# Top-k attention and a sigmoid-gated MLP in one kernel: moving a score unit, a pair of bounds, and the PSUM home of three MLP units

## The chip, the cores and the metric

The kernel runs on one core of one Trainium2 chip. The metric is the device time of one execution in microseconds (us). Engine names follow the profile: PE is TensorE, PEld its weight load, DVE is VectorE, ACT is ScalarE, POOL is GpSimd, SP issues most of the DMAs.

## The reference

```python
# q, k, v: (8, 8, 576, 64); w_in: (512, 2048); w_out: (2048, 512); all float32
scores = matmul(q, k.transpose(0, 1, 3, 2)) / sqrt(64)
kth = partition(scores, -32, axis=-1)[..., -32:-31]   # the 32nd largest of each row
scores = where(scores >= kth, scores, -1e9)
attn = exp(scores - max(scores)); attn = attn / (sum(attn) + 1e-9)
x = matmul(attn, v)                                   # -> transposed to (4608, 512)
h = x @ w_in
out = (h * sigmoid(1.702 * h)) @ w_out
```

Each row of 576 scores keeps its 32 largest values; the rest get weight zero. The attention output of all eight heads of a token is one row of the MLP's input.

## The kernel before, in words

**Slots.** A *slot* is 128 query rows of two heads. There are 8 x 18 = 144 of them. For each slot PE computes two 128x576 score tiles (`scores`, L282) into PSUM, ACT copies them to SBUF (`copy_scores`, L294), DVE finds the 32nd largest value of each row, ACT cuts the scores at that value and takes the exponential with its row sum (`exponentials`, L397 and L400), the exponentials are transposed, and PE multiplies them with v.

**Three ways through a slot.** Slots 0 to 11 search the full rows on DVE (`topk`, L304 and L307), and transpose on PE (`turn`, L448, L451), with a diagonal matrix of 1/sum as moving operand, which POOL makes (`divide`, L413). From slot 12 on (`PAIRED`) the search works on pairs: `pair_up(n)` takes the larger of each two scores on DVE (`greater`, L323) and the smaller on POOL (`lesser`, two instructions, L326 and L327), and `topk_of_pairs` searches both (L344, L347). From slot 12 on (`SETTLED`) the exponentials also leave by DMA (`split`, L470 and L472) and come back transposed by DMA (L478); the sums are inverted on DVE (`invert`, L429, L431), spread by POOL (`wide`, L433), and multiplied in after the product with v (L527, L538, L944, L552). The bounds of the exponentials come from POOL: `cut` and `low` (L388, L389) for slots below 12, `low` (L377) later.

**The MLP.** Finished blocks of 128 tokens go through it in *units*: `hidden` (L591) makes a 128x512 piece of h in one PSUM bank, `tanh` (L613, and L616 for a copy of h) reads it on ACT, `gate` multiplies on POOL (L625, L626), and `project` (L646) adds the unit's part to the block's output in another bank, `po`. When all parts are in, ACT brings it out (`leave`, L654). Where two blocks are ready, a unit is *double*: it works on both at once, with half the columns of each, and two `po` banks are in use.

**PSUM.** The banks are split into four pools: `ps_s` (scores, two tiles of two banks), `ps_t` (two banks, tag `tp`: transposes, products with v, and some units), `ps_h` (one bank, units) and `ps_p` (one bank, `po`). The second `po` of a double unit lives in `ps_h`. Which of `ps_t` and `ps_h` a unit takes is decided in `hidden`: double units, and units that come while `pos["other"]` is set, take `ps_t`, the others take what the caller says. A tile waits for the last reader of the tile that had its bank before.

**Order.** Nothing is reordered after the program: inside `manual_schedule` each engine runs its instructions in the order in which the code emits them, and waits by semaphores. `slot(n)` emits one slot (n up to 12), `two_slots(n)` emits two (n = 13, 15, 17, ...), with the search of slots n and n+1. Of a call of `two_slots` the order on PE is: `hidden`, `project`, transposes of new q and k where they are due, `sum_rows` (L527), `scores(n+2)`, products with v (L538), `scores(n+3)`, `hidden`, `project`. On ACT `copy_scores(n+2)` follows the two instructions of `tanh` and the copies of transposed q and k (L218, L222, L224). `pair_up(n+1)` sits inside the search of slot n, at its 15th instruction, so the search of slot n goes on only when the scores of slot n+1 have been copied. The call with n = 13 (`opens`) puts `scores(15)` first.

The weights of the MLP are rounded in pieces during the first twelve slots; the last instructions of a piece are two on POOL (L144, L147), emitted while the next slot searches (`finish_one`).

Of the kernel before, what the change touches and what calls it, by code (L numbers as in the profile page):

```python
# [30 lines left out]
def kernel(  # L31
# [53 lines left out]
    SETTLED = 12  # L85
    PAIRED = 12
# [19 lines left out]
    ps_t = pool("ps_t", 2, space=PSUM)  # L106
# [274 lines left out]
    def bounds(n):  # L381

        if n >= PAIRED:
            return lows(n)
        top = st[n]["top"]
        cut = st[n]["cut"] = small.tile([P, 2], F32, name="cut")
        low = st[n]["low"] = small.tile([P, 2], F32, name="low")
        nc.gpsimd.tensor_scalar(cut[:], top[:, :, TOPK - 1], -1.0, None, op0=ALU.mult)  # L388
        nc.gpsimd.tensor_tensor(out=low[:], in0=top[:, :, TOPK - 1], in1=top[:, :, 0], op=ALU.subtract)  # L389
# [182 lines left out]
            self.left = list(range(FC))  # L572
            self.done = 0

    pos = {"other": False}
    ready = []
    to_gate, gated, to_project = [], [], []

    def hidden(into=None):
        if not ready:  # L580
            return
        blocks = ready[:2]
        many = len(blocks)
        fs = blocks[0].left[: G // many]
        first, step = min(x.place for x in blocks), abs(blocks[0].place - blocks[-1].place) or 1
        blocks = sorted(blocks, key=lambda x: x.place)
        into = ps_t if many > 1 or pos["other"] else into
        ph = (into or ps_h).tile([P, G * P], F32, name="ph", tag="tp" if into else "ph")
        for i, f in enumerate(fs):
            for c in range(CC):  # L590
                nc.tensor.matmul(  # L591
                    ph[:, i * many * P : (i + 1) * many * P],
                    lhsT=win[:, c, f * P : (f + 1) * P],
                    rhs=xs[:, first : first + step * (many - 1) + 1 : step, c, :],
                    start=(c == 0),
                    stop=(c == CC - 1),
                )
        to_gate.append((ph, fs, blocks))
        for x in blocks:
            x.left = [f for f in x.left if f not in fs]  # L600
        if many > 1:
            pos["other"] = True
        while ready and not ready[0].left:
            free.append(ready.pop(0).place)
            if len(ready) < 1 or len(ready[0].left) == FC:
                pos["other"] = False
# [58 lines left out]
    in_use = []  # L665
# [121 lines left out]
    def slot(n):  # L787

        todo = later.pop(n, [])
        for fn, args in todo:  # L790
            if fn is not prepare and fn is not prepare_by_dma:
                fn(*args)
        preparing = [(fn, args) for fn, args in todo if fn is prepare or fn is prepare_by_dma]
        some = [round_piece(x) for x in by_slot.get(n, [])] if n else early
        if n == 0:
            for piece in some:
                piece["low"]()
                piece["sign"]()
        else:
            bounds(n - 1)  # L800

            exponentials(n - 1, bring_all if n % 4 == 1 else lambda: None)
            copy_scores(n + 1)
            bring_all()
            while signs:
                signs.pop(0)()
            if 1 < n <= TURNS:
                turn_main(n - 2)
                turn_ends(n - 2)
            for piece in some:  # L810
                piece["size"]()
            tanh(False)
        for i, op in enumerate(topk_of_pairs(n) if n >= PAIRED else topk(n)):
            op()
            if i == 2:
                for _ in range(min(3 if n >= TURNS else 6, len(unfinished))):
                    finish_one()
            if i == 5:
                if n > 0:
                    divide(n - 1)  # L820
                while unfinished:
                    finish_one()
            if i == 10:
                gate(False)
        for piece in some:
            piece["shift"]()
            unfinished.extend(piece["finish"])
        if n < NP:
            for fn, args in preparing:
                fn(*args)  # L830
        if n >= TURNS:
            turn_main(n - 1)
            turn_ends(n - 1)
        if n > 0:
            for piece in some:
                piece["low"]()
        scores(n + 2)
        if n == SETTLED:
            copy_scores(n + 2)
        if n == 0:  # L840
            return
        for i, piece in enumerate(some):
            if n == TURNS and i > 0:
                signs.append(piece["sign"])
            else:
                piece["sign"]()
        idle = not ready and n < TURNS
        if 1 < n <= TURNS:
            values(n - 2, put_off if n == TURNS else None)
        if n >= TURNS:  # L850
            values(n - 1, put_off)
        if n >= NP:
            for fn, args in preparing:
                fn(*args)
        if n > PROJECTS and may_project(2):
            project()
        if idle:
            stay_warm(8)
        hidden()
# [12 lines left out]
    def two_slots(n):  # L872

        first, second = [later.pop(m, []) for m in (n, n + 1)]
        live = lambda m: 0 <= m < N
        aside = n < N

        def begin(todo):
            for fn, args in todo:
                if fn is not prepare and fn is not prepare_by_dma:  # L880
                    fn(*args)

        def prepare_some(todo):
            for fn, args in todo:
                if fn is prepare or fn is prepare_by_dma:
                    fn(*args)

        def find(m):
            for i, op in enumerate(topk_of_pairs(m) if live(m) else [lambda: None] * 23):
                op()  # L890
                if i == 8 and m % 2:
                    invert(m - 2)
                if i > 1 and unfinished:
                    finish_one()

        def project_one():
            if may_project(0):
                project(True)

        def measure(m):  # L900
            if live(m):
                bounds(m)
            gate(aside)

        opens = n == SETTLED + 1
        begin(first)
        measure(n - 1)
        if opens:
            scores(n + 2)
            bring_all()  # L910
        if live(n - 1):
            exponentials(n - 1)
            split(n - 1)
        if opens:
            copy_scores(n + 2)
            tanh(aside)
        find(n)
        hidden(ps_t if opens else None)
        project_one()
        tanh(aside)  # L920
        prepare_some(first)
        held = [m for m in (n - 3, n - 2) if live(m) and "rows" in st[m]]
        o = ps_t.tile([P, 2, 2, P], F32, name="o", tag="tp") if held else None
        for i, m in enumerate(held):
            sum_rows(m, o[:, i, 0, :])
        if live(n + 2) and not opens:
            scores(n + 2)
            copy_scores(n + 2)
        leave_all()
        for i, m in enumerate(held):  # L930
            values_at(m, o[:, i, 1, :])
        if live(n - 1):
            turn_by_dma(n - 1)
        while turns:
            turns.pop(0)()
        if live(n + 3):
            scores(n + 3)
        begin(second)
        measure(n)
        def bring():  # L940
            if not held:
                return
            x = raws.tile([P, 2, 2, P], F32, name="x", tag="raw")
            nc.scalar.copy(out=x[:], in_=o[:])  # L944
            for i, m in enumerate(held):
                x_of(m, x[:, i, 1, :], x[:, i, 0, :])

        if live(n):
            exponentials(n, bring)
        else:  # L950
            bring()
        if live(n):
            split(n)
            turn_by_dma(n)
        hidden(ps_t)
        if live(n + 3):
            copy_scores(n + 3)
        tanh(aside)
        prepare_some(second)
        project_one()  # L960
        leave_all()
        find(n + 1)

    with tc.manual_schedule():
        opening()
        for n in range(SETTLED + 1):
            if n == PAIRED:
                pair_up(n)
            slot(n)
        for n in range(SETTLED + 1, N + 4, 2):  # L970
            two_slots(n)
        while ready or to_gate or gated or to_project:
            last_slot()
# [30 lines left out]
```

## Time and profile before

| what | value |
|---|---|
| median of the three runs (1479.12, 1480.97, 1481.0) | 1480.97 us |
| the profiled execution: its time, its span | 1481.2 us, 1479.4 us |
| PE, PEld busy | 1436.7 us (97%), 1019.3 us (69%) |
| DVE, ACT, POOL busy | 1331.9 (90%), 1173.7 (79%), 860.2 us (58%) |
| mean granted TensorE clock | 0.987 |
| chain that ended last, by engine | PE 89%, DVE 6%, ACT 3% |

The span runs from the first to the last instruction; the time is 1.8 us longer. "x" counts instructions, "[0.69 <-ACT ob L654]" behind a row means that the engine had been idle for 0.69 us and that the instruction of line 654 on ACT released it. A row with x32 merges 32 records, and its duration goes from the start of the first to the end of the last; matmuls overlap at their ends, so the step from one row's start to the next row's start is the cleaner measure. Slot 12 lies at about 145 to 161 us of the span, the call of `two_slots` with n = 15 at about 188 to 207 us.

### The profile page before, as it was taken

The page shows a single profiled execution, that of the slowest core. Times are in us where ns is not written, and L with a number is a line of the kernel's source. Part 1 is how long each engine was busy: PE and PEld are TensorE (multiplying, and loading weights), DVE is VectorE, ACT ScalarE, POOL GpSimd, SP SyncE. Part 2 cuts the span into 40 slices and gives each one's busy share as a digit, 9 for nine tenths or more (in the row PEclk, how much of TensorE's full clock was granted, in tenths as well). Part 3 has the DMA queues.
Part 4 walks back from the last instruction along what each step waited for, and adds up shares of the span by engine and source line. Part 5 has one row for each costly group of instructions (what it writes and reads, how often), then busy time and mean ns, then how long its engine had stood idle before and what let it go on. Part 6 is the DMA issues. An engine that isn't in the chain of part 4 may idle for free.

```text
span 1479.4 us, 29105 instructions
## 1 busy us (share of the span) xinstructions
PE 1436.7 (97%) x9696; PEld 1019.3 (69%) x9696; DVE 1331.9 (90%) x4541; ACT 1173.7 (79%) x1865; POOL 860.2 (58%) x1119
## 2 busy tenths in 40 slices
PE   7789899999999999999999999999999999999998
PEld 5667656777666667777666667777766667777665
DVE  7999889999999999999999999999999999999910
ACT  6998588878788888888878787888878788877730
POOL 3777555655666666565666666555666666565510
PEclk8899999999999999999999999999999999999999
DMA  7451256776768677676767676676777766644430
GB/s 244 135 156 52 56 155 182 201 186 172 176 185 201 168 188 183 178 187 164 183 184 202 168 181 185 176 188 171 182 177 192 201 169 186 148 124 130 129 86 15
DMA packets 516311, 242.04 MB, mean 164 GB/s; under 512 B 452672, under 2 KB 490560, under 8 KB 516160
## 3 DMA queue, kind: packets, MB, share of 16 engines
q1 hardware_dynamic: 515728, 239.89, 61.8%
q8 instruction: 76, 1.25, 0.4%
q14 instruction: 75, 0.61, 0.1%
q10 hardware_dynamic: 432, 0.30, 0.1%
HBM read 45.09 MB, written 102.24 MB: 100 GB/s over the span
## 4 chain that ended last, share of the span: by engine, by line
PE 89%; DVE 6%; ACT 3%; issue 1%; POOL 0%; POOLq 0%; DVEq 0%; ACTq 0%
PE ph L591 33%; PE po L646 32%; PE s_ps L282 11%; PE o L538 10%; DVE top L304 3%; DVE left L307 2%; PE tp L448 1%; PE o L527 1%; ACT pr L400 1%; ACT sc L294 0%; PE o L503 0%; ACT sc L397 0%; PE none L169 0%; DVE win L152 0%; DVE top L344 0%
## 5 line engine op out<-in xcount | busy, mean ns | idle before, releaser
L591 PEld LDWEIGHTS ph<-xT,win 128*128 128x128 f32 x3520 | 483.9, 191 | 90.1 <-issue 56.2
L591 PE MATMUL ph<-xT,win 128*128 128x128 f32 (+1 forms) x3520 | 537.8, 309 | 3.4 <-ACT ob L654 2.1
L646 PE MATMUL po<-wout,th 128*128 128x512 f32 x1152 | 518.4, 593 | 1.1 <-ACT ob L654 1.1
L646 PEld LDWEIGHTS po<-wout,th 128*128 128x128 f32 x1152 | 213.2, 190 | 214.5 <-issue 207.3
L344 DVE MAX8 top<-left 128x8 f32<-128x288 f32 x792 | 325.5, 446 | 0.0
L294 ACT ACTIVATE sc<-s_ps 128x576 f32<-128x576 f32 x288 | 171.2, 647 | 141.5 <-PE s_ps L282 141.5
L470 ACT COPY sc<-pr 128x2304 uint16<-128x2304 uint16 x132 | 278.8, 2112 | 4.2
L552 POOL TENSOR_TENSOR xT<-x 128x128 f32<-128x128 f32 (+1 forms) x148 | 60.8, 433 | 298.0 <-ACT x L944 298.0
L347 DVE MATCH_REPLACE8 left<-top,left 128x288 f32<-128x288 f32 x528 | 229.7, 443 | 0.0
L326 POOL TENSOR_TENSOR lesser<-sc,greater 128x576 int32<-128x576 int32 x132 | 186.3, 1411 | 71.7 <-DVE greater L323 65.9
L400 ACT ACTIVATE pr<-sc,low 128x576 f32<-128x576 f32 x288 | 221.4, 778 | 0.0
L397 ACT ACTIVATE sc<-sc,cut 128x576 f32<-128x576 f32 x288 | 208.1, 779 | 7.8 <-POOL cut L388 7.7
L344 DVE MAX8 top<-lesser 128x8 f32<-128x288 f32 x528 | 213.9, 446 | 0.0
L327 POOL TENSOR_TENSOR lesser<-lesser,sc 128x576 int32<-128x576 int32 x132 | 186.3, 1411 | 10.4
L282 PE MATMUL s_ps<-qk_t 64*128 64x288 f32 (+1 forms) x1280 | 185.0, 436 | 0.2 <-ACT qk_t L218 0.2
L626 POOL TENSOR_TENSOR th<-th,h 128x512 f32<-128x512 f32 x128 | 163.1, 1274 | 10.8 <-POOL th L625 0.2
L323 DVE TENSOR_TENSOR greater<-sc 128x576 f32<-128x576 f32 x132 | 101.0, 765 | 53.4 <-ACT sc L294 52.6
L625 POOL TENSOR_SCALAR th<-th 128x512 f32<-128x512 f32 x128 | 79.0, 617 | 120.0 <-ACT th L613 119.8
L538 PE MATMUL o<-pt,v_l 128*64 128x128 f32 (+1 forms) x2368 | 143.8, 265 | 0.0
L538 PEld LDWEIGHTS o<-pt,v_l 128*64 128x64 f32 x2368 | 120.1, 137 | 25.7 <-issue 23.6
L282 PEld LDWEIGHTS s_ps<-qk_t 64*128 64x128 f32 (+1 forms) x1280 | 100.6, 180 | 41.5 <-issue 22.5
L613 ACT ACTIVATE th<-ph 128x512 f32<-128x512 f32 x144 | 85.9, 597 | 51.1 <-PE ph L591 44.1
(83 smaller groups left out, 1461.3 us busy)
## 6 DMA issues: line engine op xcount, KB each, us to landing
rows<-sc SPq DMA_DIRECT2D x132, 576.0 KB, 3.1
qk_rows<-halves SPq DMA_DIRECT2D x48, 256.0 KB, 2.8
qk_l<-in_q_dram SPq DMA_DIRECT2D x64, 128.0 KB, 2.9
raw<-in_moe_w_in_dram SPq DMA_DIRECT2D x16, 512.0 KB, 4.6
v_l<-in_v_dram SPq DMA_DIRECT2D x32, 256.0 KB, 3.2
raw<-in_moe_w_out_dram SPq DMA_DIRECT2D x16, 512.0 KB, 3.5
out_dram<-ob SPq DMA_DIRECT2D x32, 256.0 KB, 2.8
qk_l<-in_k_dram SPq DMA_DIRECT2D x62, 128.0 KB, 2.8
```

The costliest lines, as they stand in the source:

```text
L282: nc.tensor.matmul(ps[i][rows, c, 0:HALF], lhsT=qT[b, hps[p]][on, cols], rhs=kT[b, hps[p]][on, FIRST[i] + c * HALF : FIRST[i] + (c + 1) * ...
L294: nc.scalar.mul(out=to, in_=ps[i][:, :, 0:HALF], mul=SCALE)
L326: nc.gpsimd.tensor_tensor(out=whole, in0=a.bitcast(I32), in1=greater[n][:].bitcast(I32), op=ALU.subtract)
L327: nc.gpsimd.tensor_tensor(out=whole, in0=whole, in1=b.bitcast(I32), op=ALU.add)
L344: nc.vector.max(found(r, i, True), src[:, i, :])
L347: nc.vector.match_replace(to[:, i, :], found(r, i), src[:, i, :], LOWEST)
L397: nc.scalar.activation(sc[:, i, :], sc[:, i, :], AF.Prelu, bias=cut[:, i : i + 1], alpha=HUGE)
L400: nc.scalar.activation(pr[:, i * S : (i + 1) * S], sc[:, i, :], AF.Exp, bias=low[:, i : i + 1], accum_out=den[:, i : i + 1],)
L470: nc.scalar.copy(out=halves, in_=pr[:].bitcast(U16).rearrange("p (k h) -> p h k", h=2))
L538: nc.tensor.matmul(o[j * D : (j + 1) * D, cols], lhsT=main[:, j, c, :] if c < NF else tail[:, j, :], rhs=pt[:, MAIN[j] + c if c < NF else ...
L591: nc.tensor.matmul(ph[:, i * many * P : (i + 1) * many * P], lhsT=win[:, c, f * P : (f + 1) * P], rhs=xs[:, first : first + step * (many - ...
L646: nc.tensor.matmul(x.po[:], lhsT=gT[:, i * P : (i + 1) * P], rhs=wout[:, f, :], start=(x.done == 0), stop=(x.done == FC - 1))
```

## The change

Four edits.

1. `pair_up(12)` moves from ahead of `slot(12)` to behind `bounds(11)` in it. On POOL `cut` and `low` of slot 11 now stand ahead of the two instructions of `lesser` of slot 12. No other engine's order changes by it.
2. In the call of `two_slots` with n = 15, as already in that with n = 13, `scores(17)` stands ahead of the first MLP unit on PE, and `copy_scores(17)` ahead of `tanh` on ACT. (Before, on PE, it stood between `sum_rows` and the products with v.)
3. In the same call the inversion of the sums (`invert`) stands behind the 14th instead of the 9th instruction of slot 15's search on DVE, next to `pair_up(16)`.
4. In `hidden` a unit takes `ps_t` also when `ps_h` holds a `po`, and so do the next units after it or after a double one, by a counter `pos["rest"]` that is set to 2. In the order of the instructions this changes the bank of three units in all: in three places the single unit that follows the last unit of a pair of blocks, with the sequence `ph` in `ps_t`, `po` in `ps_h`, `ph`, `po` in `ps_p`, has its `ph` in `ps_t` instead of `ps_h`.

No instruction is added or removed, and no DMA is moved.

```diff
-    pos = {"other": False}
+    pos = {"other": False, "rest": 0}
...
-        into = ps_t if many > 1 or pos["other"] else into
+        if many > 1 or pos["other"] or "ps_h" in in_use:
+            pos["rest"] = 2
+        elif pos["rest"]:
+            pos["rest"] -= 1
+        into = ps_t if pos["rest"] else into
...
             bounds(n - 1)
+            if n == PAIRED:
+                pair_up(n)
...
-                if i == 8 and m % 2:
+                if i == (13 if m < SETTLED + 4 else 8) and m % 2:
                     invert(m - 2)
...
         opens = n == SETTLED + 1
+        ahead = n < SETTLED + 4
         begin(first)
         measure(n - 1)
+        if ahead:
+            scores(n + 2)
         if opens:
-            scores(n + 2)
             bring_all()
         if live(n - 1):
             exponentials(n - 1)
             split(n - 1)
+        if ahead:
+            copy_scores(n + 2)
         if opens:
-            copy_scores(n + 2)
             tanh(aside)
...
-        if live(n + 2) and not opens:
+        if live(n + 2) and not ahead:
             scores(n + 2)
             copy_scores(n + 2)
...
         for n in range(SETTLED + 1):
-            if n == PAIRED:
-                pair_up(n)
             slot(n)
```

## The prediction

> **What bounds the kernel now.** I read the page first: PE is busy 97% of the span and makes 89% of the chain that ended last. Then I split the span into stretches. From 240 us on PE has no hole except in a few stretches, and one of these is 560 to 600 us (columns: stretch, length, then busy us and count of PE, PEld, DVE, ACT, POOL, then clock, DMA share, GB/s):
>
> ```profile
> PE 89%; DVE 6%; ACT 3%; issue 1%; POOL 0%; POOLq 0%; DVEq 0%; ACTq 0%
> ...
> 520.00:560.00 40.00, 40.00 (x273) 28.09 (x272) 37.80 (x135) 33.92 (x53) 25.39 (x36) 1.00 0.73 182
> 560.00:600.00 40.00, 39.31 (x286) 28.61 (x286) 37.49 (x134) 31.25 (x49) 23.96 (x31) 1.00 0.72 194
> 600.00:640.00 40.00, 40.00 (x287) 29.08 (x286) 37.75 (x135) 35.55 (x54) 23.98 (x33) 1.00 0.68 181
> ```
>
> So from about 235 us to the end the time is PE's work plus its few waits: what PE gains before 235 us, or in a wait after it, stays to the end; what another engine gains is worth only what PE waits for it. The list of waits, limited to 235 to 1400 us, gives PE just two entries (total us, times, longest):
>
> ```profile
> PE ph L591 <- ACT ob L654: 2.1, 3, 0.7
> PE ph L591 <- POOL xT L552: 1.1, 1, 1.1
> ```
>
> The first is what edit 4 is about. Before 235 us PE has real holes, in slot 12 and in the calls of `two_slots` from 195 to 230 us.
>
> **Edit 4, the three units.** PE's order of time around the first place, and ACT's one row that releases it:
>
> ```profile
> 557.82 3.84 PE L591 MATMUL ph<-xT,win 128*128 128x128 f32 x32
> ...
> 576.92 3.84 PE L591 MATMUL ph<-xT,win 128*128 128x128 f32 x32
> 580.60 3.60 PE L646 MATMUL po<-wout,th 128*128 128x512 f32 x8
> 584.88 3.84 PE L591 MATMUL ph<-xT,win 128*128 128x128 f32 x32 [0.69 <-ACT ob L654]
> ...
> 596.98 3.84 PE L591 MATMUL ph<-xT,win 128*128 128x128 f32 x32
> ...
> 584.23 0.60 ACT L654 ACTIVATE ob<-po 128x512 f32<-128x512 f32 x1 [2.01 <-PE po L646]
> ```
>
> The `po` at 580.60 is the last in `ps_h`; the next `ph` wants the same bank and waits until ACT has brought the block out. The round 557.82 to 576.92 takes 19.10 us, the round with the wait, 576.92 to 596.98, 20.06 us: 0.96 us dearer (0.84 later start, and 0.11 for the first matmuls after a wait). The other two places, 919.50 to 939.56 and 1262.08 to 1282.14 us, are 20.06 us as well. In `ps_t` the unit takes the bank of the product with v, whose reader L944 ended at 576.5 us, 7.5 us before PE gets there (584.04 without the wait). What is late next? The following L527 (591.99, about 591.0 then) now wants the bank of the `ph` of 576.92, read by ACT until 582.2: 8.8 us of slack. The unit after that, at about 596.0, wants the bank of the moved `ph`, which ACT reads until 590.8: 5 us. Neither DVE nor ACT is the limit of that round: DVE waits 0.42 and 1.75 us in it for copies of scores, which wait for PE. So 3 x 0.96 = **2.9 us** off; bounds 2.1 (only the idle itself) and 2.9.
>
> **Edit 1, slot 12.** In order of time on ACT, POOL and PE:
>
> ```profile
> 146.44 1.41 POOL L326 TENSOR_TENSOR lesser<-sc,greater 128x576 int32<-128x576 int32 x1 [5.80 <-ACT raw L153]
> 149.31 0.21 POOL L388 TENSOR_SCALAR cut<-top 128x2 f32<-128x2 f32 x1
> 149.55 1.44 ACT L397 ACTIVATE sc<-sc,cut 128x576 f32<-128x576 f32 x2 [3.11 <-POOL cut L388]
> 152.23 1.28 POOL L144 TENSOR_TENSOR wout<-wout,raw 128x512 int32<-128x512 int32 x1
> 153.91 0.72 POOL L413 TENSOR_SCALAR xT<-ident,rden 128x128 f32<-128x128 f32 x2 [0.40 <-DVE rden L410]
> 154.33 3.78 PE L448 MATMUL tp<-xT,pr 128*128 128x128 f32 x16 [4.48 <-POOL xT L413]
> ```
>
> `cut` and `low` need only DVE's search of slot 11, which ends at 145.0, and POOL is idle then: they run at 145.0 to 145.8 (0.64 + 0.19 us, as at 133.54), ahead of the 146.44 at which `lesser` can start, so `lesser` is not delayed (0.6 us of slack). ACT's 3.1 us wait goes: exponentials at 146.4. DVE's division, which waits for their sums, ends at 150.5 instead of 153.7. But PE waits for POOL's diagonal (L413), and POOL has `lesser` (to 149.3) and three instructions of the last weight pieces ahead of it. These start 0.32 us earlier, where `cut` and `low` stood, and end at 153.2 instead of 153.5; the 0.40 us wait for DVE goes too. So L413 starts at 153.2, PE at 153.6: **0.7 us** off, not 3.1. Bounds: 0.3 (if the 0.40 comes back as latency) and 3.1 (were POOL's pieces not in the way). DVE's 3 us lead is waited away at slot 16's scores: its 0.93 us wait for ACT at 186.50 becomes about 3.
>
> The clock is in play here. PE stood still from 149.85 to 154.33 (4.48 us), and the granted clock was then 0.50 from 154 to 160 us: L448 took 3.78 us for 1.95 at full clock (slot 11's row), L451 0.70 for 0.44, the scores 2.11 for 1.24, 3.0 us dearer in all. The Trainium skill ("TensorE: Matmul & The Clock Gate", Part 1) says that the clock is halved after at least one idle window of about 3.4 us, with windows that run free. The gap shrinks to 3.8 us, and a whole idle window fits into it in only (3.8 - 3.4)/3.4, about 1 of 9 phases, so by that rule most executions would keep the clock, and the edit would be worth 0.7 + 3.0 = 3.7 us. The trace speaks against it: a gap of only 2.63 us was followed by a slow stretch too, 2.53 us for the same 16 matmuls and a clock of 0.83 over the stretch.
>
> ```profile
> 104.45 2.53 PE L448 MATMUL tp<-xT,pr 128*128 128x128 f32 x16 [2.63 <-POOL xT L413]
> 100.00:110.00 10.00, 7.37 (x53) 5.80 (x53) 9.96 (x24) 9.35 (x20) 8.02 (x8) 0.83 0.44 142
> 150.00:160.00 10.00, 5.67 (x26) 4.83 (x28) 7.42 (x24) 5.67 (x13) 7.04 (x8) 0.68 0.00 1
> ```
>
> I go by the row: 3.8 us still costs the clock. Bounds for it: 0 and 3.0 us off.
>
> **Edits 2 and 3, the call with n = 15.**
>
> ```profile
> 195.00 0.60 ACT L613 ACTIVATE th<-ph 128x512 f32<-128x512 f32 x1 [0.94 <-PE po L646]
> 198.81 1.19 ACT L294 ACTIVATE sc<-s_ps 128x576 f32<-128x576 f32 x2 [1.39 <-PE s_ps L282]
> 200.11 0.76 DVE L323 TENSOR_TENSOR greater<-sc 128x576 f32<-128x576 f32 x1 [4.62 <-ACT sc L294]
> ```
>
> The scores of slot 17 are ready on PE at 189.0 instead of 198.7, and ACT copies them when `split` ends, at 194.1 to 195.2, most of it in the 0.94 us in which it waited anyway. So DVE's 4.62 us wait goes. For PE the edit is a swap. Steps: scores 1.17, unit after scores 3.67 (557.82 to 561.49) where the unit after a `po` took 3.57, `project` 3.43. So `project` ends at 187.80 + 1.17 + 3.67 + 3.43 = 196.07 instead of 194.80; `tanh`, which waits for that `project`, starts 1.27 later, and with it the copies of q and k and L527, which waits for them: 198.47 instead of 197.20. There the scores are missing (1.17), so the products with v end at 198.47 + 0.34 + 2.49 = 201.30 instead of 201.20: **0.1 us** dearer. ACT's L944 waits for that end as before (201.31), so ACT, though it has 1.1 us of copies less to do after 198, goes on when it did. And nobody waits for DVE: from 200 to 230 us PE waits for ACT (L654 1.13 us, L218 0.89, 1.85 and 0.25), and ACT, without a hole from 198.81 to 213.5, for PE. The one row that names DVE's heir is L527 at 213.24, 0.25 us "POOL low", but ACT's copy L218 ended at 213.1 as well, so at most 0.25 us is there. Bounds: 0.25 off, 0.3 dearer. Edit 3 delays `wide` by nothing: DVE waited 1.05 us for the sums at 183.26, and in the new place it arrives at about 181 (edit 1's lead) and waits for the same sums; `wide` is wanted by PE 14 us later. If that cover went, it would cost its 0.35 us.
>
> **Sum.** 1481.2 us (profiled, span 1479.4) - 2.9 - 0.7 + 0.1 = 1477.7. The median of the three runs is 0.2 lower, so **1477.5 us**. A difference under about 0.2% (3.0 us) can't be told from none; the forecast is just beyond it.
>
> **Rivals.** *The clock stays up in slot 12*, or DVE's lead is worth something to PE: 3.0 us more, 1474.5. For it the skill's rule, against it the 2.63 us gap. *Only edit 4 works*, PE's 0.7 us in slot 12 being eaten by ACT or POOL before 235 us: 1480.97 - 2.8 = 1478.2, no difference to be told. For it: ACT is full from 198.81. Against it: its start there is PE's. *The three waits are replaced by others* (ACT or DVE set the rounds once PE is quicker): edit 1 alone is left, 1480.4. Against it DVE's waits of 0.42 and 1.75 us. *Slower*: `copy_scores(17)` now stands ahead of `tanh` and of the copies PE waits for, and it writes the buffer of slot 13's scores, which must first have left by DMA. That was issued at 185.40 and landed 2.8 us later, 188.2; ACT gets there at 193.3. Were it late, ACT, then PE, would wait with it: from a landing at about 194.5 on each us costs one, and past 198 it has eaten the 3.5 us. A landing at 203 would give 1486. The trace has nothing like it: 2.8 to 3.8 us for these DMAs.
>
> **How the numbers follow.** The likeliest case 0.66 (its own range 1476.3 to 1478.6: edit 4 from 2.1 to 2.9, edit 1 from 0.3 to 1.5, and the spread of the runs, 1.9 us); clock or lead 0.10 (1473.5 to 1475.5); only edit 4 0.12; replaced waits 0.06; slower 0.06. Range 1474.3 to 1479.8: below it a third of the clock case and below 0.06, above it the last two. Faster by over 0.2% (below 1478.0): 0.50 of the first case's 0.66, and the second's 0.10: 0.60. Within: the rest of the first, 0.16, the third and fourth, 0.34. Slower 0.06.
>
> **What will show it.** Right: no PE wait for ACT L654 after 235 us and three rounds of 19.1 instead of 20.06 us; ACT's L397 of slot 11 at 146.4, L413 at 153.2 and PE at 153.6 with the clock at 0.5 behind it; DVE's wait at slot 17 gone, and PE at 235.3 in the old profile arriving 0.6 us earlier. Wrong: PE at that point more than 2 us earlier (clock or DVE), or later than before (slot 15), or a wait of PE for ACT L613 or L616 in the three rounds.

## The result: 1475.54 us, 0.2% faster

| | median | lowest to highest | runs |
|---|---|---|---|
| before, run beside it | 1478.45 us | 1477.88 to 1481.0 | 11 |
| after | 1475.54 us | 1472.79 to 1478.4 | 11 |

The ratio of after to before is 0.998, with a 95% interval of 0.997 to 0.9989: about 2.9 us off, with an interval of 1.6 to 4.4 us. The profiled execution took 1475.54 us, its span 1473.8 us at a clock of 0.990; the one before had 1479.4 us of span at 0.987. These two spans differ by 5.6 us, which is more than the medians differ; why is worked out below.

**Still PE to the end.** The chain of the changed kernel, and its stretches of 40 us in the same columns as before:

```profile
PE 89%; DVE 5%; ACT 3%; issue 2%; DMA 1%; POOL 0%; POOLq 0%; ACTq 0%; SPq 0%
...
560.00:600.00 40.00, 40.00 (x282) 28.69 (x281) 37.91 (x137) 32.20 (x52) 24.85 (x32) 1.00 0.69 190
240.00:280.00 40.00, 39.82 (x289) 29.04 (x289) 39.62 (x138) 33.38 (x51) 24.28 (x32) 1.00 0.79 205
```

The hole of 0.69 us at 560 to 600 us is gone. There is a new small one at 240 to 280. PE's waits from 230 to 1400 us are now these two:

```profile
PE ph L595 <- POOL xT L552: 1.1, 1, 1.1
PE o L538 <- DMA pt<-rows: 0.2, 1, 0.2
```

The line numbers of the MLP have moved by four (L591 is L595 now, L646 is L650, L654 is L658). No wait for the block brought out by L658 is left in this stretch, and the first wait is the old one. The second is new.

**The three rounds.** PE around the first of the three places:

```profile
555.00 3.84 PE L595 MATMUL ph<-xT,win 128*128 128x128 f32 x32
...
574.11 3.84 PE L595 MATMUL ph<-xT,win 128*128 128x128 f32 x32
577.78 3.60 PE L650 MATMUL po<-wout,th 128*128 128x512 f32 x8
581.22 3.73 PE L595 MATMUL ph<-xT,win 128*128 128x128 f32 x32
...
593.22 3.84 PE L595 MATMUL ph<-xT,win 128*128 128x128 f32 x32
```

The round 555.00 to 574.11 takes 19.11 us and the round 574.11 to 593.22, which waited before, 19.11 us as well. The other two places give 915.74 to 934.84 (19.10) and 1257.36 to 1276.47 (19.11). The unit at 581.22 starts 3.44 us behind its predecessor, without a pause.

**Slot 12.** ACT, POOL and PE in order of time:

```profile
145.01 0.31 POOL L388 TENSOR_SCALAR cut<-top 128x2 f32<-128x2 f32 x1 [4.42 <-DVE top L304]
146.25 1.45 ACT L397 ACTIVATE sc<-sc,cut 128x576 f32<-128x576 f32 x2
146.41 1.41 POOL L326 TENSOR_TENSOR lesser<-sc,greater 128x576 int32<-128x576 int32 x1 [0.76 <-ACT raw L153]
149.27 1.29 POOL L144 TENSOR_TENSOR wout<-wout,raw 128x512 int32<-128x512 int32 x1
150.64 1.28 POOL L147 TENSOR_TENSOR wout<-wout,raw 128x512 f32<-128x512 f32 x1
151.88 1.29 POOL L144 TENSOR_TENSOR wout<-wout,raw 128x512 int32<-128x512 int32 x1
153.14 1.23 POOL L413 TENSOR_SCALAR xT<-ident,rden 128x128 f32<-128x128 f32 x2
153.58 3.68 PE L448 MATMUL tp<-xT,pr 128*128 128x128 f32 x16 [3.77 <-POOL xT L413]
157.19 0.44 PE L451 MATMUL tp<-xT,pr 128*64 128x128 f32 x4
157.56 1.24 PE L282 MATMUL s_ps<-qk_t 64*128 64x288 f32 x8
```

ACT no longer waits for `cut`, and its exponentials run 3.3 us earlier. PE gets only 0.75 us of that: POOL is full from 146.41 on, and the diagonal (L413) stands behind `lesser` and three instructions of the weight pieces. The matmuls behind the gap run at half clock as before (3.68 us for 16), but the clock came back sooner this time: L451 and the scores ran at full clock.

**The call with n = 15.** DVE at the scores of slots 16 and 17, and PE where it goes on behind the call:

```profile
184.51 0.76 DVE L323 TENSOR_TENSOR greater<-sc 128x576 f32<-128x576 f32 x1 [2.85 <-ACT sc L294]
193.42 0.74 DVE L323 TENSOR_TENSOR greater<-sc 128x576 f32<-128x576 f32 x1
199.41 1.24 PE L282 MATMUL s_ps<-qk_t 64*128 64x288 f32 x8
```

The 4.62 us wait at slot 17 is gone (193.42 has no bracket). The lead is waited away at slot 16's scores, 2.85 us where it was 0.93.

**Where the 5.6 us of the two profiles went.** The starts of the same PE rows in both:

| row | before | after | gain so far |
|---|---|---|---|
| slot 12's transposes, L448 | 154.33 | 153.58 | 0.75 |
| product with v behind them, L503 | 160.71 | 158.73 | 1.98 |
| scores behind the call with n = 15, L282 | 201.20 | 199.41 | 1.79 |
| `sum_rows` at about 228, L527 | 228.70 | 226.91 | 1.79 |
| first unit behind it, L591/L595 | 235.29 | 231.93 | 3.36 |
| end of the span | 1479.4 | 1473.8 | 5.6 |

0.75 us is the edit in slot 12, 1.23 us the clock that came back sooner, and 0.2 us goes in the call with n = 15. The step of 1.57 us at 228 to 232 us is the clock again: in the profile of before, L527 took 0.63, the scores 2.29 and the first products 1.40 us there, where the changed kernel has 0.41, 1.24 and 1.09. The three changed bank places are worth 2.86 us (20.06 us each to 19.11, 19.10, 19.11), and 0.56 us is lost again in two rounds of 19.51 and 19.26 us (246.04 to 265.55 to 284.81), where PE waited for DMAs. The sum is 0.75 + 1.23 - 0.19 + 1.57 + 2.86 - 0.56 = 5.66 us. The clock's share of it, 2.8 us, turns out to differ from execution to execution; on what it depends is shown further down.

### The profile page after: what moved, and what is told of

Read it like the earlier page. It is cut to its first block, busy times and chain, and to the rows that moved or that the text cites. A ratio compares the mean times of both kernels' runs of the same rounds, so it can differ in the third digit from the quotient of the medians.

```text
span 1473.8 us, 29103 instructions
## 1 busy us (share of the span) xinstructions
PE 1433.5 (97%) x9696; PEld 1017.8 (69%) x9696; DVE 1333.4 (90%) x4541; ACT 1173.9 (80%) x1865; POOL 862.9 (59%) x1119
## 3 DMA queue, kind: packets, MB, share of 16 engines
q8 instruction: 76, 1.25, 0.4%
## 4 chain that ended last, share of the span: by engine, by line
PE 89%; DVE 5%; ACT 3%; issue 2%; DMA 1%; POOL 0%; POOLq 0%; ACTq 0%; SPq 0%
PE ph L595 33%; PE po L650 32%; PE s_ps L282 10%; PE o L538 10%; DVE top L304 3%; DVE left L307 2%; PE tp L448 1%; PE o L527 1%; ACT pr L400 1%; ACT sc L397 0%; ACT sc L294 0%; PE o L503 0%; DMA pt<-rows 0%; PE none L169 0%; DVE win L152 0%
## 5 line engine op out<-in xcount | busy, mean ns | idle before, releaser
L595 PEld LDWEIGHTS ph<-xT,win 128*128 128x128 f32 x3520 | 484.1, 191 | 86.8 <-issue 57.5
L595 PE MATMUL ph<-xT,win 128*128 128x128 f32 (+1 forms) x3520 | 537.6, 309 | 1.4 <-POOL xT L552 1.2
L650 PE MATMUL po<-wout,th 128*128 128x512 f32 x1152 | 518.4, 593 | 1.1 <-ACT ob L658 1.1
L650 PEld LDWEIGHTS po<-wout,th 128*128 128x128 f32 x1152 | 213.2, 190 | 214.5 <-issue 207.4
L397 ACT ACTIVATE sc<-sc,cut 128x576 f32<-128x576 f32 x288 | 208.2, 779 | 3.4 <-POOL cut L388 3.3
L282 PE MATMUL s_ps<-qk_t 64*128 64x288 f32 (+1 forms) x1280 | 183.1, 433 | 0.2 <-ACT qk_t L218 0.2
L282 PEld LDWEIGHTS s_ps<-qk_t 64*128 64x128 f32 (+1 forms) x1280 | 99.6, 178 | 41.4 <-issue 22.7
L617 ACT ACTIVATE th<-ph 128x512 f32<-128x512 f32 x144 | 86.0, 597 | 50.8 <-PE ph L595 43.4
```

The source lines that it names most:

```text
L282: nc.tensor.matmul(ps[i][rows, c, 0:HALF], lhsT=qT[b, hps[p]][on, cols], rhs=kT[b, hps[p]][on, FIRST[i] + c * HALF : FIRST[i] + (c + 1) * ...
L397: nc.scalar.activation(sc[:, i, :], sc[:, i, :], AF.Prelu, bias=cut[:, i : i + 1], alpha=HUGE)
L595: nc.tensor.matmul(ph[:, i * many * P : (i + 1) * many * P], lhsT=win[:, c, f * P : (f + 1) * P], rhs=xs[:, first : first + step * (many - ...
L650: nc.tensor.matmul(x.po[:], lhsT=gT[:, i * P : (i + 1) * P], rhs=wout[:, f, :], start=(x.done == 0), stop=(x.done == FC - 1))
```

## The experiments

A ratio is always to the kernel before, in runs beside it: median 1479.56 us over 26 runs for the three parts alone and for the first kernel with POOL's order, 1479.95 us over 9 runs for the other four.

### The parts alone

**Edit 4 alone** (before, with the new rule for the banks):

```diff
-        into = ps_t if many > 1 or pos["other"] else into
+        if many > 1 or pos["other"] or "ps_h" in in_use:
+            pos["rest"] = 2
+        elif pos["rest"]:
+            pos["rest"] -= 1
+        into = ps_t if pos["rest"] else into
```

> Edit 4 alone on the kernel before. My theory: PE up to about 575 us as before (L527 at 228.7, first unit after it at 235.3, give or take the clock), no wait of PE for ACT L654 after 235 us, the three rounds at 19.1 instead of 20.06 us, so 2.9 us faster (ratio 0.998). Rival, waits replaced: the three rounds stay near 20 us with another releaser, time as before.

Measured: 1476.73 us (1474.98 to 1479.47, 10 runs), ratio 0.998 with an interval of 0.9971 to 0.9989, so 2.9 us off (1.6 to 4.3). From 228 us on no round is longer than 19.14 us, and PE waits nowhere for L658. By the medians this is as much as the whole change gives.

**Edit 1 alone:**

```diff
             bounds(n - 1)
+            if n == PAIRED:
+                pair_up(n)
...
         for n in range(SETTLED + 1):
-            if n == PAIRED:
-                pair_up(n)
             slot(n)
```

> Edit 1 alone on the kernel before. My theory: ACT L397 of slot 11 at 146.3 instead of 149.55, POOL L413 at 153.2 and PE L448 at 153.6 (0.7 us earlier) because the weight pieces on POOL stand in the way, clock at 0.5 after it; 0.7 us faster, plus or minus what the clock's phase gives (up to 1.5), the three rounds still 20.06. Rival, the wait for ACT was all there was: PE at 151, 3 us faster.

Measured: 1479.2 us (1476.7 to 1481.14, 11 runs), ratio 0.9992 (0.9983 to 1.0), so 1.2 us off (0 to 2.5). POOL and PE in slot 12:

```profile
145.68 1.41 POOL L326 TENSOR_TENSOR lesser<-sc,greater 128x576 int32<-128x576 int32 x1
152.38 0.72 POOL L413 TENSOR_SCALAR xT<-ident,rden 128x128 f32<-128x128 f32 x2
152.81 3.78 PE L448 MATMUL tp<-xT,pr 128*128 128x128 f32 x16 [4.09 <-POOL xT L413]
156.53 0.70 PE L451 MATMUL tp<-xT,pr 128*64 128x128 f32 x4
157.15 2.08 PE L282 MATMUL s_ps<-qk_t 64*128 64x288 f32 x8
```

PE's gap is 0.39 us shorter than before (4.48). That understates the edit. PE was further ahead of POOL in this execution: `lesser` started 0.79 us behind PE's unit (L591, 144.89) and not 0.43 us as before (146.01), and the gap holds this lead. POOL's own way, from the start of `lesser` to the diagonal, leaves it out: 7.47 us before (146.44 to 153.91), 6.70 us here, 6.73 us in the changed kernel. So the edit takes 0.74 to 0.77 us from it. The clock stays low for as long as before here (L451 0.70, the scores 2.08), so the edit alone does not bring it back sooner. The three rounds stay at 20.06 us.

**Edits 2 and 3 alone:**

```diff
-                if i == 8 and m % 2:
+                if i == (13 if m < SETTLED + 4 else 8) and m % 2:
                     invert(m - 2)
...
+        ahead = n < SETTLED + 4
         begin(first)
         measure(n - 1)
-        if opens:
+        if ahead:
             scores(n + 2)
+        if opens:
             bring_all()
...
-        if opens:
+        if ahead:
             copy_scores(n + 2)
+        if opens:
             tanh(aside)
...
-        if live(n + 2) and not opens:
+        if live(n + 2) and not ahead:
```

> Edits 2 and 3 alone on the kernel before. My theory: DVE's 4.6 us wait at slot 17 is gone, yet PE's scores of slot 18 come 0.1 us later than before (201.3), and PE at the first unit after 230 us is where it was but for the clock: time the same (within 1 us). Rival, DVE's lead is worth something: PE after 230 us 1 us or more earlier with the same clock, and the time with it.

Measured: 1480.9 us (1478.68 to 1482.99, 11 runs), ratio 1.0005 (0.9996 to 1.0014): nothing that can be told from none. DVE's wait at slot 17 is gone in this profile too. From the `project` ahead of the call (L646, 183.86) to the scores behind it (200.89) PE takes 17.03 us, as in the changed kernel (182.38 to 199.41), and 16.84 before (184.36 to 201.20). The three parts multiply to 0.998 x 0.9992 x 1.0005 = 0.9977, the whole is 0.998: as far as these intervals tell, they add up, and none needs another.

**Edit 3 alone undone** (the changed kernel with the inversion back behind the 9th instruction; one execution):

```diff
-                if i == (13 if m < SETTLED + 4 else 8) and m % 2:
+                if i == 8 and m % 2:
```

> The changed kernel without edit 3 (the inversion back at its old place in slot 15's search). My theory: DVE waits about 3 us for the sums of slot 13 inside the search instead of at its end, the search of slot 15 and slot 16's pair end when they did, PE's L527 of slot 12 and 13 stays at 196.6 (give or take the clock before it). Rival: PE's rows from 195 us on come later by 0.3 us or more against its scores of slot 17.

Measured: 1475.89 us. What changes in this call is the size of DVE's two waits:

```profile
181.06 0.17 DVE L429 TENSOR_SCALAR sums<-sums 128x4 f32<-128x4 f32 x1 [1.28 <-ACT pr L400]
184.29 0.76 DVE L323 TENSOR_TENSOR greater<-sc 128x576 f32<-128x576 f32 x1 [0.93 <-ACT sc L294]
```

With edit 3 the inversion stands behind the search instructions and waits 1.14 us (181.28), and `greater` waits 2.85 us (184.51). Without it, more of the search lies between the two waits, and they are 1.28 and 0.93 us. In both, `greater` of slot 16 starts when ACT's copy has landed, at 184.3 to 184.5 us, and PE goes from the scores of slot 17 to L527 in 10.68 us in both. Edit 3 moves the place in which DVE idles and is worth nothing to PE here.

### What holds the diagonal in slot 12

The prediction gave edit 1 only 0.7 us of ACT's 3.1 because POOL's weight pieces stand ahead of the diagonal. If that is the reason, letting the diagonal go first must release the rest. In the changed kernel the three POOL instructions of the weight pieces that slot 12 issues behind the third step of the search now follow the diagonal, with the fourth, behind the sixth step; none is left out:

```diff
-            if i == 2:
+            if i == 2 and n < PAIRED:
                 for _ in range(min(3 if n >= TURNS else 6, len(unfinished))):
```

> The changed kernel, and in slot 12 the diagonal (L413) ahead of the weight pieces on POOL (three POOL instructions of 1.28 us change places with it). Theory that POOL's pieces hold PE there: L413 at 149.7, PE's L448 at 150.1 instead of 153.6, PE idle under 0.5 us, the clock stays at 1.0 and L448 takes 1.95 us instead of 3.7: PE 5.2 us earlier at slot 13's scores than in the changed kernel, and 3 to 5 us faster than it (ratio to before 0.995 to 0.996), less if DMAs after 235 us come too late for PE. Rival, DVE's division or ACT hold PE: L448 stays above 152 us, no gain over the changed kernel.

Measured: 1470.75 us (1469.83 to 1471.59, 5 runs), ratio 0.9939 (0.9927 to 0.9951). Against the changed kernel's own ratio that is 0.9939 / 0.998 = 0.9959, some 6 us; the medians are 4.8 us apart, the upper end of what was expected. POOL and PE in slot 12:

```profile
146.38 1.42 POOL L326 TENSOR_TENSOR lesser<-sc,greater 128x576 int32<-128x576 int32 x1 [0.76 <-ACT raw L153]
147.88 1.41 POOL L327 TENSOR_TENSOR lesser<-lesser,sc 128x576 int32<-128x576 int32 x1
149.79 0.72 POOL L413 TENSOR_SCALAR xT<-ident,rden 128x128 f32<-128x128 f32 x2 [0.49 <-PE ph L595]
150.21 2.05 PE L448 MATMUL tp<-xT,pr 128*128 128x128 f32 x16 [0.43 <-POOL xT L413]
152.20 0.44 PE L451 MATMUL tp<-xT,pr 128*64 128x128 f32 x4
```

PE starts 3.37 us earlier (150.21 against 153.58), and with a gap of 0.43 us the clock stays at 1.00: the transposes take 2.05 instead of 3.68 us. Together these are 5.0 us, and L527 of the call with n = 15 is 5.0 us earlier too (191.59 against 196.59). The diagonal now waits for PE itself (0.49 us for the unit, L595). It beats both kernels.

**The same order without edit 1** (the kernel before with that one line; one execution):

> The kernel before with only the diagonal ahead of the weight pieces on POOL, and the pair of slot 12 still ahead of the bounds (edit 1 not made). My theory, two covers over the same wait: the division waits for the exponentials until 153.6 as before, L413 at 153.6, PE at 154.0: 0.3 us, so that neither half alone gives the 3.5 us which both give together. Rival: L413 at 150 or 151 already here.

Measured: 1478.86 us. POOL and PE:

```profile
146.11 1.40 POOL L326 TENSOR_TENSOR lesser<-sc,greater 128x576 int32<-128x576 int32 x1 [5.46 <-DVE greater L323]
152.74 0.72 POOL L413 TENSOR_SCALAR xT<-ident,rden 128x128 f32<-128x128 f32 x2 [3.40 <-DVE rden L410]
153.16 3.44 PE L448 MATMUL tp<-xT,pr 128*128 128x128 f32 x16 [4.11 <-POOL xT L413]
```

Now POOL is free and waits 3.40 us for DVE's division, whose sums come from ACT's exponentials, late because of `cut`. PE's gap shrinks by 0.37 us, but here too PE was further ahead of POOL (0.89 us). From the start of `lesser` to the diagonal it is 6.63 us against 7.47 before, so the order alone takes 0.84 us from POOL's way and not the 0.3 that was expected: the first instruction of the division (L408, 128x2) took 0.17 us, where it took 0.99 us before. In the six profiles in which it started while POOL ran a piece it took 0.99 to 1.27 us, in the other four 0.17.

So two chains end within half a microsecond of each other ahead of the diagonal, and removing either one (edit 1: 0.7 to 0.8 us; the order alone: 0.8 us) shows the other. With both removed the diagonal comes 3.41 us behind the start of `lesser`: 4.1 us are gone (PE's gap of 4.48 becomes one of 0.43) and, with them, the low clock.

**That order without edits 2 and 3:** the changed kernel with the line of POOL's order, and `scores(17)`, `copy_scores(17)` and `invert` in their old places.

> Edits 1 and 4, and the diagonal ahead of the weight pieces on POOL, without edits 2 and 3. If edits 2 and 3 are worth nothing (my theory: 0.1 us dearer): PE as in the kernel with all four, 0 to 0.7 us faster than it (ratio to before 0.993 to 0.994), DVE's wait at slot 17 back at 4 us or more. Rival, DVE's lead is needed once PE is earlier: PE waits longer between 185 and 230 us, 1 us or more slower than with all four.

Measured: 1471.0 us (1469.37 to 1471.95, 5 runs), ratio 0.9939 (0.9925 to 0.9953), the same as with them. Edits 2 and 3 are worth nothing when PE arrives 5 us earlier, either. DVE's wait at slot 17 is back, at 2.76 us and not the 4 us or more that were expected, and from 165 to 285 us PE has no wait that names DVE.

### What the clock costs

The changed kernel with 12 matmuls of the identity with itself (24 records in the profile) in the gap of slot 12. They write a bank that nobody reads; nothing of the computation is left out:

```diff
+        if n == PAIRED:
+            junk = ps_t.tile([P, 512], F32, name="junk", tag="tp")
+            for i in range(12):
+                nc.tensor.matmul(junk[:, 0:P], lhsT=ident[:], rhs=ident[:], start=True, stop=True)
```

> The changed kernel with twelve matmuls of the identity, which nobody reads, into a bank of ps_t in the hole ahead of slot 12's transposes (2.9 us of PE work where PE stands still for 3.7). It measures the clock by itself. If the slow stretch is the price of the hole: L448 still starts at 153.6, the clock stays at 1.0, L448 takes 1.95 instead of 3.7 us, and slot 13's PE work is 1.3 to 3 us earlier than in the changed kernel (ratio to before 0.996 to 0.997). If the slow stretch has nothing to do with the hole: L448 stays at 3.7 us and the time at that of the changed kernel.

Measured: 1472.82 us (1472.68 to 1473.51, 5 runs), ratio 0.9952 (0.9939 to 0.9964), so 0.28% below the changed kernel by the ratios (4.1 us) and 2.7 us by the medians; the upper end of the expectation or beyond it. PE in slot 12:

```profile
148.91 2.84 PE L840 MATMUL junk<-ident 128*128 128x128 f32 x24
153.51 2.05 PE L448 MATMUL tp<-xT,pr 128*128 128x128 f32 x16 [1.76 <-POOL xT L413]
155.49 0.44 PE L451 MATMUL tp<-xT,pr 128*64 128x128 f32 x4
```

The transposes start when they did (153.51 against 153.58) and take 2.05 us instead of 3.68. From L448 to the product with v behind it (L503) PE takes 3.52 us here (153.51 to 157.03), 5.15 in the changed kernel (153.58 to 158.73) and 6.38 before (154.33 to 160.71). So the low clock behind slot 12's gap costs 1.6 and 2.9 us in these two profiles, and 2.7 us between the medians.

The five runs of this kernel lie within 0.8 us of each other, five of the one with POOL's order within 1.8 us, eleven of the changed kernel within 5.6 us. Of these eleven the fastest (1472.79 us) had the highest mean granted clock, 0.991, and the slowest (1478.4 us) the lowest, 0.986; with edit 1 alone it was 0.991 at 1476.7 us and 0.986 at 1481.14. The clock thus goes with most of the scatter; how much of that is slot 12's share was not separated.

## Why the prediction was right, point by point

The prediction was 1477.5 us, in a range of 1474.3 to 1479.8; the median is 1475.54 us, and the ratio's whole interval lies below one. Against 1478.45 us, the median of the eleven runs of before, the forecast gain of 3.5 us stands beside 2.9 measured. The absolute time is 2 us off since its base, the median of three runs (1480.97 us), was 2.5 us too high: the spread that was put down to the runs, 1.9 us, was taken from three of them, and is 3.1 us over eleven and 4.5 us over 26. The times confirm edit 4 and the sum; they are too coarse for the smaller terms, 0.7 us for edit 1 and 0.1 us for edits 2 and 3, which rest on the traces.

**Edit 4, 2.9 us: right, and shown.** Alone it gives 2.9 us (1.6 to 4.3); each of the three rounds went from 20.06 to 19.11 us, and no new wait of PE, for L617, L620 or a bank of `ps_t`, came in their place. What was said to be late next (8.8 and 5 us of slack) was not. That rules out the rival in which the waits are replaced.

**Edit 1, 0.7 us: right in place and size.** L397 at 146.25 (forecast 146.4), L413 at 153.14 (153.2), PE at 153.58 (153.6). The reason, POOL's pieces ahead of the diagonal, is shown by the kernel that takes them away, and 3.1 us, the upper bound "were POOL's pieces not in the way", was too small for what that is worth. The step that was mis-sized there is the bound: it left out that a gap without the pieces would be so short that the clock stays up.

**The clock: the row was right, the use of the rule not.** In all ten profiles the granted clock changes only at the ends of windows of 3.41 us, which follow each other without a break through an execution. These are the windows of slot 12, first of the profile of before, then of that of after (columns: stretch, length, then busy us and count of PE, then clock, DMA share, GB/s):

```profile
150.23:153.64 3.41, 0.00 (x0) 1.00 0.00 0
153.64:157.06 3.42, 2.73 (x13) 0.50 0.01 2
157.06:160.47 3.41, 3.41 (x17) 0.50 0.00 0
...
150.22:153.64 3.42, 0.06 (x1) 1.00 0.01 2
153.64:157.05 3.41, 3.41 (x16) 0.50 0.00 0
157.05:160.46 3.41, 3.41 (x35) 1.00 0.00 0
```

The Trainium skill ("TensorE: Matmul & The Clock Gate", Part 1) gives free-running windows of about 3.4 us, and these rows agree with that. By its rule an idle window halves the clock. The prediction read this as a window in which PE stands still from end to end, and so got its 1 in 9. That reading does not hold. From 65 to 1400 us, each of the 19 windows in which PE was busy for 1.45 us or less was followed by half clock, and none in which it was busy for 1.55 us or more. (In the first 65 us the border is less sharp: seven windows of 1.5 to 2.0 us were followed by half clock, others as busy were not.) A gap of 3.77 us leaves at most about 1.5 us of work in the busier case, an estimate in which a boundary between two windows halves the gap: 3.41 - 3.77/2 = 1.52. So a low clock behind it was to be expected nearly always, not rarely, and the rival "the clock stays up" falls.

The step "3.8 us still costs the clock, the same 3.0" is only roughly right: it cost 2.9 us in the profile of before and 1.6 in that of after. In both a window happens to begin at 153.64 us. After the change PE starts again at 153.58, fills that window, and has full clock from 157.05. Before, it starts at 154.33, leaves 0.69 us of that window empty, and gets full clock one window later, at 160.47. So in this pair the edit's 0.75 us decided, by the luck of where the windows lay. With edit 1 alone PE starts 0.75 us into a window (152.81, the window from 152.06), and the clock costs 2.8 us again.

**Edits 2 and 3, 0.1 us dearer: right.** In the trace of the changed kernel and in that of the two edits alone PE lost 0.19 us in the call, within the bound of 0.3, and alone the two have a ratio of 1.0005 (0.9996 to 1.0014). The wait that vanished was DVE's, for which PE didn't wait. The lead that DVE had from edit 1 was waited away at slot 16's scores, as forecast.

**The slower rival did not come about.** ACT's copy of slot 17 found its buffer free (no wait at 191.99). At 236.49 and 256.70 us ACT does wait for DMAs of this kind, in calls whose order the change leaves alone:

```profile
236.49 1.19 ACT L294 ACTIVATE sc<-s_ps 128x576 f32<-128x576 f32 x2 [1.32 <-DMA rows<-sc]
256.70 1.19 ACT L294 ACTIVATE sc<-s_ps 128x576 f32<-128x576 f32 x2 [2.08 <-DMA rows<-sc]
```

The profile of before has no such wait, but that of edit 4 alone has (0.46 and 1.56 us), and that of the kernel before with POOL's order has longer ones (2.10 and 3.34 us). So edits 2 and 3 are not needed for them. PE has no wait for ACT there.

**What the list of signs missed.** "PE at 235.3 arriving 0.6 us earlier" came out as 3.36 us, which the prediction would have read as "clock or DVE". It was the clock, at two places (1.23 and 1.57 us), one of which (228 us) the prediction had not seen. The rest, 0.56 us, is what it had forecast.

## What to carry to other kernels

When a small instruction releases the critical engine, look at everything that ends just before it, on every queue it passes: here two chains ended within 0.5 us of each other, so removing one alone brought it forward by 0.7 to 0.8 us, and removing both by 4.1 us, which kept the clock up too. A wait on an engine that nobody waits for is worth nothing, even at 4.62 us; a wait of 0.69 us on the engine that bounds the kernel is worth its 0.96 us each time. And one pair of profiles is no measure of a change of 0.2%: here it said 5.6 us, and the medians 2.9.

## What the runs showed of the hardware

**Short gaps also cost clock, and where they lie decides.** PE's pause of 1.85 us ahead of L221 at about 228 us, with 0.25 us more behind it, is the same to 0.01 us in all ten profiles. It is followed by half clock in three of them. In the kernel with POOL's order:

```profile
221.34 0.33 PE L221 MATMUL tp<-ident,qk_l 128*128 128x128 f32 x1 [1.86 <-ACT qk_t L218]
...
218.44:221.85 3.41, 1.37 (x10) 1.00 0.45 92
221.85:225.26 3.41, 3.34 (x16) 0.50 1.08 203
```

and in that of edits 2 and 3 alone:

```profile
227.82 0.33 PE L221 MATMUL tp<-ident,qk_l 128*128 128x128 f32 x1 [1.86 <-ACT qk_t L218]
...
224.56:227.97 3.41, 1.55 (x11) 1.00 0.37 145
227.97:231.38 3.41, 3.02 (x33) 1.00 1.09 239
```

What differs is how much of the pause falls into one window of 3.41 us. In the three with half clock (before, edit 1 alone, POOL's order) PE was busy for 1.31, 1.31 and 1.37 us of the emptiest window there, and the round from L527 to the next L527 takes 20.7 us. In the other seven it was busy for 1.55 to 2.15 us, and the clock stayed at 1.00; the round takes 19.13 us in the changed kernel. A pause of 1.76 us right behind the extra matmuls (2.13 us busy in its window) was not followed by half clock either. So a border between 1.45 and 1.55 us separates all of these cases. PE's busy time is modelled in the profile, so the border is known no better than that.

**DMA issues of varying length.** In the changed kernel PE waited for transposed exponentials (L478) that came late at 249 us. SP's queue some 20 us ahead of it, and PE:

```profile
229.98 2.53 SPq L184 DMA_DIRECT2D qk_l<-in_k_dram  x2
...
249.02 1.09 PE L538 MATMUL o<-pt,v_l 128*64 128x128 f32 x16 [0.18 <-DMA pt<-rows]
```

The first row is SP's issue of two loads of k; the stores and transposes of the exponentials stand behind it in the same in-order queue. It takes 1.28 us in the profile of before and 2.53 us here. Five profiles have long rounds behind such issues:

| kernel | issues that were longer | rounds lose | ACT's longest wait for a store |
|---|---|---|---|
| changed | 2.53 us for 1.28 | 0.56 us | 2.08 us |
| POOL's order without edits 2 and 3 | 1.69 for 0.63, 2.04 for 1.27 | 1.34 | 2.48 |
| edits 2 and 3 alone | 1.64 for 1.28, 1.25 for 0.63 | 1.06 | 2.61 |
| edit 3 undone | 2.02 for 1.28, 2.00 for 1.27 | 1.17 | 2.72 |
| POOL's order without edit 1 | 2.24 for 1.28, 2.22 for 1.15 | 1.87 | 3.34 |

The others lose nothing there, with edit 4 alone (an issue of 1.74 for 1.28), with POOL's order (1.75 for 1.28) and with the filled gap (1.41 for 0.63), and ACT waits for a store for 1.56 us at most. So the length of one issue does not decide by itself; the waits for the stores, which stand in the same queue, order the profiles better. The loss comes with and without edits 2 and 3, so it is not their doing. What makes an issue long was not tested and stays open.
